# Stage one of a Fourier mixer on full rows: class r = 0 over 94 partitions, feature 128 from a padded matrix, front pieces one slot earlier, the last half tile in its own PSUM bank

## The chip, the cores and the metric

The kernel runs on one NeuronCore of a Trainium2 chip. The metric is the device time of one execution in microseconds. Before the change the median of three runs is 602.24 us (602.23 to 602.45).

## What is computed

The reference, cut to what matters:

```python
def _attn_ref(x):                                # x: (8, 3008, 256)
    X = np.fft.fft(x, axis=1)
    X = np.fft.fft(X, axis=2)
    return X.real.astype(np.float32)

def _moe_ref(x, w_tok1, w_tok2, w_ch1, w_ch2):   # d_tok 256, d_ch 1536
    h = np.maximum(x.transpose(0, 2, 1) @ w_tok1, 0.0) @ w_tok2
    u = x + h.transpose(0, 2, 1)
    h2 = np.maximum(u @ w_ch1, 0.0) @ w_ch2
    return (u + h2).astype(np.float32)
```

The input of the second function is the output of the first. Eight batches are worked on, one after the other; the whole computation is in 16-bit floats on the tensor engine (PE) with 32-bit sums in PSUM.

## The kernel before

**Two halves of work per batch.** The *front* of a batch makes the Fourier transform and the token mixer and ends in the tiles `ut` (the activations u, transposed). The *channel part* multiplies `ut` by the two channel matrices. While the channel part of batch b runs, the front of batch b + 1 is run in small pieces between its matmuls. The order on every engine is the order in which the program is written; nothing is rescheduled.

**The channel part** goes in six chunks of 512 positions per batch (the last has 448), and each chunk in four *slots*, s = 0 to 3. A slot has number 4c + s, from 0 to 23, and holds: three pairs of first channel matmuls (`mm1`, L763, into PSUM tiles `pc`, six matmuls of 512 or 448 columns; ACT takes them out with a ReLU, L766), and one quarter of the second channel product of the chunk before (`mm2`). Most chunks do `mm2` with a form of Strassen's scheme (`mm2_sums`, L804): its PSUM tiles are `px` and `py`, groups of 12 matmuls of 128 columns; `keep(i)` copies a part of px to `m` on ACT (L809); `residual` adds products and the input on the DVE or on POOL (L789); `block_sums` makes sums of blocks on the DVE (L780). A chunk at the end of an even batch, the first chunk and the very last one are *plain* (L863, PSUM tile `po`). The last tile of all is done in two halves of 128 columns so that the first half can be added and stored earlier; both halves lie in one `po` tile.

**The front** is a generator, and every `next` runs one piece. For batches 1 to 7 the pieces are, in order: six of `inner` (stage one for classes r = 1 to 15, five matmuls of 96 columns each, L511), two of `outer` (the edge pieces: class r = 0 by `edge`, L576 and L579, and class 16, L520), twelve of stage two (one `w` group each: L589 and L590 into `pw`, taken out by ACT, L307, and by the DVE, L592), two of `tok1` (L606, one for each half of the token features, with `units` on the DVE, L617 to L620, and `relu` on ACT, L629), `third(0)` (L638; `qs` on ACT, L641; two DVE operations into `yt`, L645), and then the pieces that make `ut`: two of `pu` (L723, added on the DVE, L731) for each chunk, and `third(1)` and `third(2)` in between. Numbered from 1 they are: 1 to 6 inner, 7 and 8 edges, 9 to 20 `w`, 21 and 22 `tok1`, 23 `third(0)`, 24 and 25 `pu` of chunk 0, 26 `third(1)`, 27 and 28 `pu` of chunk 1; the remaining nine run in the next iteration under `own_plan`.

`plan[b][slot]` says how many front pieces of batch b + 1 run in a slot. The first half of them (rounded down; none in a slot with s = 1) goes between `mm1` and `mm2`, the rest after `mm2`. `fold_plan` does the same for `fold`, the twelve DVE steps per batch that add the mirrored input rows and columns and fill the tile `eo` (L457 to L465) two batches ahead. Front pieces use a ring of three PSUM banks (tag "f"), `mm1` another three ("mm"), px, py and po the remaining two ("o2").

**Stage one.** `eo` has 94 partitions (`KR`; 47 is `NQ`): 47 for even and 47 for odd input groups. The tables `t1n` and `t1b` hold cosines and sines; in `t1n` the first part is masked by `mask0`, which is 1 on the first 47 partitions and 0 on the others. Class r = 0 needs only the first 47 rows, and the second feature half of the folded input needs, in its first output row, feature 128 in place of a zero. Before, `edge` takes both by slicing: 47 rows of `eo`, and a product with one single column (partition 0 of the output). Batch 0 has its own stage one (`fold0`, `zw0`, table `t0h`, L537).

Of the kernel before, what the change touches and what calls it, by code (L numbers as in the profile page):

```python
# [41 lines left out]
def kernel(  # L42
# [49 lines left out]
    def pvec(name, dt=FP32):  # L92
        return const.tile([P, 1], dt, tag=name, name=name)
# [249 lines left out]
    for o, h in ((shift0, half[0]), (shift1, half[1])):  # L343
        nc.vector.scalar_tensor_tensor(out=o[:], in0=h[:], scalar=-S / 4.0, in1=quart[:],
                                       op0=AT.mult, op1=AT.mult)
    mask0, q24 = pvec("mask0"), pvec("q24")
    ts(mask0[:], xicol[:], -1.0, AT.mult, 1.0, AT.add)
    ts(q24[:], qcol[:], 24.0, AT.add)
    t1n = const.tile([KR, 2, 2, 24], FP16, tag="t1n")
    t1b = const.tile([KR, 3, 24], FP16, tag="t1b")  # L350
# [4 lines left out]
    cs, v1 = (gen.tile([KR, 5, 24], FP32, tag=n, name=n) for n in ("cs", "v1"))  # L355
    reduced(v1[:], m1[:], m1[:], 47)
    sin(cs[:], m1[:], 47)
    t0h = gen.tile([NQ, 2, 24], FP16, tag="t0h")
    nc.scalar.activation(out=t0h[:], in_=cs[0:NQ, 0:4:2, :], func=AFT.Copy, scale=0.5)
    rest_of(vp, mp, S)  # L360
    table3(tp, vp)
    ident = const.tile([P, P], FP16, tag="ident")
# [4 lines left out]
    acol = pvec("acol")  # L367
    ts(acol[:], pcol[:], -1.0, AT.mult, 127.0, AT.add)
    ts(anti[:], jrow[:, 0:P], acol[:], AT.is_equal)
    for i, m in ((0, mask0), (1, xicol)):  # L370
        ts(t1n[:, :, i, :], cs[:, i:4:2, :], m[0:KR, :], AT.mult)
    ts(t1b[:, 1, :], cs[:, 4, :], float(np.sqrt(0.5)), AT.mult,
       xicol[0:KR, :], AT.mult)
    nc.vector.tensor_copy(out=t1b[:, 0:3:2, :], in_=t1n[:, :, 0, :])
    ixc = const.tile([P, 1], I32, tag="ixc")
    cfeat = pvec("cfeat")
    ts(cfeat[:], pcol[:], 1.0, AT.is_lt, -128.0, AT.mult)
# [19 lines left out]
    def tables_folded():  # L397
        pl.tensor_copy(out=td0[:], in_=tdu[:, 0:131])
        ts(td0[0:1, :], td0[0:1, :], 0.5, AT.mult, eng=pl)
        pl.tensor_copy(out=td1[:], in_=tdu[:, 131:WD])  # L400
        pl.memset(td1[0:1, 0:1], 0.5)
        pl.tensor_copy(out=alt[:], in_=altu[:, 0:131])
        pl.memset(alt[:, 130:131], 0.0)

    tcol, sgn = pvec("tcol"), pvec("sgn")
    perm = const.tile([P, P], FP16, tag="perm")
# [40 lines left out]
    def fold(b, engs):  # L447
        xp, xm = x_tiles.pop(b)
        eo = perb.tile([KR, NR, D], FP16, tag="eo", name="eo")
        state[b] = {"eo": eo}  # L450
        add, sub = AT.add, AT.subtract
        for s, (t0, t1) in enumerate(((13, 17), (9, 13), (5, 9), (1, 5))):
            tt = engs[s].tensor_tensor
            t = slice(t0, t1)
            rv = slice(16 - t0, 16 - t1 if t1 < 17 else None, -1)
            if s == 0:
                tt(out=xp[:, 1:NR, 0], in0=xp[:, 1:NR, 0], in1=xm[0:KR, ::-1, 0], op=add)  # L457
                tt(out=eo[:, :, 0], in0=xp[:, :, 0], in1=xp[:, :, 0], op=add)
            tt(out=xp[:, t, 1:D], in0=xp[:, t, 1:D], in1=xm[0:KR, rv, D - 1:0:-1], op=add)
            yield  # L460
            if t0 == 1:
                t = slice(0, t1)
            tt(out=eo[:, t, 1:129], in0=xp[:, t, 1:129], in1=xp[:, t, 255:127:-1], op=add)
            yield
            tt(out=eo[:, t, 129:256], in0=xp[:, t, 1:128], in1=xp[:, t, 255:128:-1],  # L465
               op=sub)
            yield


    def fold0():  # L470
        xp, xm = x_tiles.pop(0)
        eo = perb.tile([KR, NR, D], FP16, tag="eo", name="eo")
        state[0] = {"eo": eo, "xp": xp}
        tt, add = nc.vector.tensor_tensor, AT.add

        def mirror(t0, t1, lo, hi):
            rv = slice(16 - t0, 16 - t1 if t1 < 17 else None, -1)
            rd = slice(D - lo, D - hi if lo else None, -1) if lo else 0
            c = slice(lo, hi) if lo else 0
            t = slice(t0, t1)  # L480
            tt(out=xp[:, t, c], in0=xp[:, t, c], in1=xm[0:KR, rv, rd], op=add)

        r = slice(0, NQ)
        for t0 in (13, 9, 5, 1):
            if t0 in (13, 5):
                mirror(t0 - 4, t0 + 4, 0, 1)
            mirror(t0, t0 + 4, 1, D)
            yield
            if t0 == 13:
                nc.vector.memset(eo[r, 1, 0:1], 0.0)  # L490
                tt(out=eo[r, 0, 0:1], in0=xp[r, 0, 0:1], in1=xp[r, 0, 0:1], op=add)
                for i, op in ((0, add), (1, AT.subtract)):
                    tt(out=eo[r, i, 1:D], in0=xp[r, 0, 1:D], in1=xp[r, 0, D - 1:0:-1],
                       op=op)
                yield
# [34 lines left out]
    def zw0():  # L530
        st = state[0]
        eo, xp = st["eo"], st["xp"]
        z = perb.tile([P, 2, 24, 64], FP16, tag="z", name="z")

        def edge(pz, c):
            for i in range(2):
                nc.tensor.matmul(pz[:, 0:24], lhsT=eo[0:NQ, i, c], rhs=t0h[:, i, :],  # L537
                                 start=(i == 0), stop=(i == 1))

        for t0, e in Z0_ORDER:  # L540
            for half in range(2):
                if t0:
                    inner(xp, t0, half, z_put(z, half, t0, e[half]), ps_any)
                else:
                    outer(xp, half, z_put(z, half, 0, e[half]), edge,
                          ps_any)
                yield
        w = st["w"] = perb.tile([P, NG, WD], FP16, tag="w", name="w", bufs=2)
        for g in range(NG):
            pw = ps_any("pw")  # L550
            for lo, hi in ((131, WD), (0, 131)):
                for i, tab in ((0, tdu), (1, tdb)):
                    nc.tensor.matmul(  # L553
                        pw[:, lo:hi],
                        lhsT=z[:, i, 2 * g:2 * g + 2, :].rearrange("p a b -> p (a b)"),
                        rhs=tab[:, lo:hi], start=(i == 0), stop=(i == 1))
            copy(W0_COPY[g], w[:, g, :], pw[:, 0:WD])
            yield
# [4 lines left out]
    def front(b):  # L563
        st = state[b]
        if b == 0:
            yield from rest(b)
            return
        eo = st["eo"]
        z = perb.tile([P, 2, 24, 64], FP16, tag="z", name="z")
        for t0 in (11, 6, 1):  # L570
            for half in range(2):
                inner(eo, t0, half, z_put(z, half, t0, 0))
                yield
        for half in range(2):
            def edge(pz, c):
                nc.tensor.matmul(pz[:, 0:24], lhsT=eo[0:NQ, 0, c],  # L576
                                 rhs=t1n[0:NQ, half, 0, :], start=True, stop=True)
                if half:
                    nc.tensor.matmul(pz[0:1, 0:24], lhsT=eo[0:NQ, 0, P:P + 1],  # L579
                                     rhs=t1n[0:NQ, 0, 0, :], start=True, stop=True)  # L580

            outer(eo, half, z_put(z, half, 0, 0), edge)
            yield
        w = st["w"] = perb.tile([P, NG, WD], FP16, tag="w", name="w", bufs=2)
        for g in range(NG):
            pw = ps_f("pw")
            za = z[:, 0, 2 * g:2 * g + 2, :].rearrange("p a b -> p (a b)")
            zb = z[:, 1, 2 * g:2 * g + 2, :].rearrange("p a b -> p (a b)")
            nc.tensor.matmul(pw[:, 131:WD], lhsT=zb, rhs=td1[:], start=True, stop=True)  # L589
            nc.tensor.matmul(pw[:, 0:131], lhsT=za, rhs=td0[:], start=True, stop=True)  # L590
            copy(0, w[:, g, 132:WD], pw[:, 132:WD])
            nc.vector.scalar_tensor_tensor(  # L592
                out=w[:, g, 0:131], in0=alt[:], scalar=pw[:, 131:132],
                in1=pw[:, 0:131], op0=AT.mult, op1=AT.add)
            yield
        yield from rest(b)
# [247 lines left out]
    def mm2(b, c, c1, ks, box):  # L844
# [14 lines left out]
        o = D * (ks % 2)  # L859
        w = P if final and ks == 3 else D  # L860
        for d in range(0, D if n else 0, w):
            for ct in range(NCT):
                nc.tensor.matmul(po[0:n, o + d:o + d + w],  # L863
                                 lhsT=c1[:, ct, ks * P:ks * P + n],
                                 rhs=wc2[:, ct, d:d + w],
                                 start=(ct == 0), stop=(ct == NCT - 1))
            if final and ks == 3:
                j, p = ((lower, lower), (upper, turned_))[d // w]
                residual(nc.vector, osb[:, 3, j], po[:, o + d:o + d + w], rt[:, 3, p])
# [84 lines left out]

    plan = [[0] * 10 + [2] * 10 + [1, 2, 2, 3]] + [[1] * 13 + [0] + [2, 1] * 5] * (BB - 1)
    own_plan = [[2, 1, 1, 1, 1, 1, 1, 0, 1, 1, 0, 0, 1, 1] + [0] * 10,
                [1, 1, 1, 0, 0, 1, 1, 0, 1, 1, 0, 0, 1, 1] + [0] * 10]
    own_plan += [[1, 1, 1, 0, 0, 1, 1, 0, 1, 1, 0, 0, 1, 1] + [0] * 10] * (BB - 2)  # L960
    early_plan = [0] * 4 + [2, 2, 1, 2, 1, 2, 2] + [0] * 13
    fold_plan = [[0] * 8 + [1, 2, 0, 0] * 4 for _ in range(BB)]
    fold_plan[0] = [0] * 16 + [2, 2, 1, 0, 2, 2, 0, 0]
    fold_plan[1] = [1, 2, 0, 0] + [0] * 4 + [0, 2, 0, 0] + [1, 2, 0, 0] * 2 + [1, 2, 1, 0]
    prev = None
    turned_u = {(0, 0): turn_u(0, 0)}
    for b in range(BB):
# [90 lines left out]
```

## Time and profile before

| | before |
|---|---|
| median of three runs | 602.24 us |
| profiled execution | 602.5 us |
| span of its instructions | 600.7 us |
| granted TensorE clock | 0.998 |
| matmuls | 6325, busy 588.6 us |
| DVE busy | 449.7 us |
| ACT busy | 436.5 us |
| POOL busy | 141.2 us |

The span is counted from the first to the last instruction; the profiled execution has 1.8 us more around it. The busy time of matmuls overlaps, since they are pipelined, so the distance between the starts of neighbours says more than their duration. All times of places in the trace are microseconds from the start of the span. Iteration 0 runs up to about 102 us, and each further one takes about 71 us.

### The profile page before, as it was taken

What the parts mean: (1) busy time and instruction counts of PE and PEld (TensorE: products, weight loads), DVE (VectorE), ACT (ScalarE), POOL (GpSimd) and SP (SyncE); (2) the same over time, 40 slices, a digit from 0 to 9 for tenths busy, and PEclk for the clock granted to TensorE, in tenths of its full rate; (3) what the DMA queues carried; (4) which work ended last, traced back from release to release, by engine and by line L of the source; (5) the groups of instructions that cost most, each with busy time, mean ns of one, the idle gap of its engine ahead of it and who ended that gap; (6) DMA issues with size and microseconds to landing.
All of it is one profiled execution on the core that took longest, in us unless ns stands there. A gap on an engine that the chain in (4) does not pass through costs nothing.

```text
span 600.7 us, 15716 instructions
## 1 busy us (share of the span) xinstructions
PE 588.6 (98%) x6325; PEld 421.7 (70%) x6325; DVE 449.7 (75%) x1022; ACT 436.5 (73%) x984; POOL 141.2 (23%) x234
## 2 busy tenths in 40 slices
PE   6999999999999999999999999999999999999997
PEld 4846677667776677767777667766777777766675
DVE  8878697668796887659888687757879667676572
ACT  8776976777768777686777776777676867767772
POOL 7601322311142121311133112401211121111131
PEclk9999999999999999999999999999999999999999
DMA  9996961883539233953429432582232424233433
GB/s 149 211 182 126 137 98 38 153 122 53 87 61 174 54 76 67 152 72 88 73 50 165 96 64 55 98 160 53 55 89 46 81 53 97 47 70 70 83 60 100
DMA packets 86681, 56.53 MB, mean 94 GB/s; under 512 B 54944, under 2 KB 83552, under 8 KB 85856
## 3 DMA queue, kind: packets, MB, share of 16 engines
q1 hardware_dynamic: 77984, 37.77, 34.8%
q0 software_dynamic: 8320, 17.49, 17.0%
q8 instruction: 49, 0.80, 0.6%
q10 hardware_dynamic: 304, 0.26, 0.2%
q14 instruction: 24, 0.20, 0.1%
HBM read 34.98 MB, written 24.64 MB: 99 GB/s over the span
## 4 chain that ended last, share of the span: by engine, by line
PE 94%; DVE 3%; ACT 2%; issue 0%; POOL 0%; DVEq 0%; POOLq 0%
PE pc L763 40%; PE px L804 23%; PE py L804 9%; PE pu L723 7%; PE po L863 4%; PE pt L606 4%; PE pz L511 2%; PE py L638 1%; PE pq L638 1%; PE pw L589 1%; PE pw L590 1%; ACT z L307 1%; PE pw L553 0%; DVE sb L780 0%; ACT tt L307 0%; PE ph L428 0%
## 5 line engine op out<-in xcount | busy, mean ns | idle before, releaser
L766 ACT ACTIVATE c<-pc 128x512 f16<-128x512 f32 (+1 forms) x572 | 295.9, 595 | 36.6 <-PE pc L763 21.9
L789 POOL TENSOR_TENSOR osb<-osb,rt 128x256 f32<-128x256 f32 x84 | 78.9, 940 | 365.8 <-DVE osb L789 358.4
L763 PE MATMUL pc<-ut,wc1p 128*128 128x512 f16 x576 | 140.6, 379 | 0.5 <-DVE ut L305 0.5
L804 PEld LDWEIGHTS <-c 128*128 128x128 f16 x2016 | 121.4, 98 | 20.4 <-issue 1.2
L763 PE MATMUL pc<-ut,wc1m 128*128 128x512 f16 (+1 forms) x576 | 134.9, 370 | 0.0
L731 DVE TENSOR_TENSOR ut<-pu,yt 128x512 f16<-128x512 f32 (+1 forms) x94 | 63.3, 674 | 46.8 <-PE pu L723 46.0
L804 PEld LDWEIGHTS <-sb 128*128 128x128 f16 x1512 | 89.9, 98 | 10.3 <-issue 0.3
L809 ACT ACTIVATE m<-px 128x256 f32<-128x256 f32 x126 | 48.5, 385 | 66.2 <-PE px L804 43.5
L763 PEld LDWEIGHTS <-wc1p 128*128 128x128 f16 x576 | 52.1, 98 | 50.3 <-issue 2.5
L763 PEld LDWEIGHTS <-wc1m 128*128 128x128 f16 x576 | 52.9, 98 | 46.5
L804 PE MATMUL px<-wst,c 128*128 128x128 f16 x1008 | 70.0, 219 | 0.0
L804 PE MATMUL px<-wc,c 128*128 128x128 f16 x1008 | 63.1, 219 | 0.7 <-DVE osb L789 0.7
L780 DVE TENSOR_TENSOR sb<-sb,c 128x768 f16<-128x768 f16 x84 | 51.2, 609 | 2.9
L307 ACT ACTIVATE z<-pz 128x480 f16<-128x480 f32 (+1 forms) x60 | 39.7, 676 | 16.9 <-PE pz L511 11.0
L789 DVE TENSOR_TENSOR osb<-py,m 128x256 f32<-128x256 f32 x84 | 35.2, 419 | 21.4 <-ACT m L809 19.4
L723 PE MATMUL pu<-w2p,uu 128*128 128x512 f16 (+1 forms) x168 | 49.8, 379 | 0.0
L780 DVE TENSOR_TENSOR sb<-c 128x768 f16<-128x768 f16 x84 | 47.2, 561 | 2.4 <-ACT c L766 2.4
L780 DVE TENSOR_TENSOR c<-c 128x768 f16<-128x768 f16 x84 | 48.1, 572 | 0.0
L780 DVE TENSOR_TENSOR sb<-c,sb 128x768 f16<-128x768 f16 x84 | 47.1, 561 | 0.0
L592 DVE SCALAR_TENSOR_TENSOR w<-alt,pw 128x131 f16<-128x131 f16 x84 | 29.4, 351 | 20.2 <-ACT w L307 20.2
L645 DVE TENSOR_TENSOR yt<-py,qs 128x512 f16<-128x512 f32 x48 | 30.9, 686 | 17.7 <-ACT qs L641 17.6
L804 PE MATMUL py<-wc,sb 128*128 128x128 f16 x504 | 35.0, 219 | 0.0
(193 smaller groups left out, 673.7 us busy)
## 6 DMA issues: line engine op xcount, KB each, us to landing
out_dram<-osb SPq DMA_DIRECT2D x83, 256.0 KB, 3.9
xp<-in_x_dram POOLq DMA_DIRECT2D x16, 272.0 KB
out_dram<-osb SPq DMA_DIRECT2D x11, 192.0 KB, 3.9
xp<-in_x_dram POOLq DMA_DIRECT2D x16, 127.5 KB
rt<-ut SPq DMA_TRANSPOSE x96, 3.9
w2s<-in_moe_w_tok_dram POOLq DMA_DIRECT2D x1, 1504.0 KB
w1p<-in_moe_w_tok_dram POOLq DMA_DIRECT2D x4, 192.0 KB
wc<-in_moe_w_ch_dram POOLq DMA_DIRECT2D x1, 768.0 KB
```

The source lines that it names most:

```text
L307: nc.scalar.activation(out=out_, in_=in_, func=AFT.Copy)
L592: nc.vector.scalar_tensor_tensor(out=w[:, g, 0:131], in0=alt[:], scalar=pw[:, 131:132], in1=pw[:, 0:131], op0=AT.mult, op1=AT.add)
L606: nc.tensor.matmul(pt[:, o:o + n], lhsT=hw[:, g, th * P:th * P + P], rhs=w[:, g, f:f + n], start=(g == 0), stop=(g == NG - 1))
L645: nc.vector.tensor_tensor(out=yt[:, h, CW * c:CW * c + CW], in0=py[:], in1=qs[:], op=op)
L723: nc.tensor.matmul(pu[:, 0:n], lhsT=uu[:, th, int(minus), h, :], rhs=w2_cols(b, c)[:, th], start=(th == 0), stop=(th == 1))
L731: nc.vector.tensor_tensor(out=ut[:, h, 0:n].rearrange("p (a b) -> p a b", b=64), in0=pu[:, 0:n].rearrange("p (b a) -> p a b", b=64), in1=y ...
L763: nc.tensor.matmul(pc[:, 0:n], lhsT=wc[:, h, ct * P:(ct + 1) * P], rhs=ut[:, h, 0:n], start=(h == 0), stop=(h == 1))
L766: nc.scalar.activation(out=c1[:, ct, 0:n], in_=pc[:, 0:n], func=AFT.Relu)
L780: nc.vector.tensor_tensor(out=o, in0=x, in1=y, op=op)
L789: eng.tensor_tensor(out=o, in0=x, in1=y, op=AT.add)
L804: nc.tensor.matmul(o[:, t], lhsT=a(k)[:, f:f + P], rhs=w(k), start=(first and t == 0 and k == 0), stop=(k == HC - 1), skip_group_check=True)
L809: nc.scalar.activation(out=m[:, i], in_=pa[:, 0], func=AFT.Copy)
```

## The change

`edge` uses all 94 rows of `eo`, where the masked table `t1n` has zeros in the rows that don't belong to class 0 (for batch 0 the table `t0h` gets such a mask, `mask0h`, which is 0.5 or 0). Feature 128 is copied into column 0 of a matrix `nyq` that is otherwise zero, its place in `eo` is cleared, and a full matmul with `nyq` is summed into the same PSUM columns. The plan of the front pieces for batches 2 to 7 puts pieces 14 to 26 one slot (some half a slot) earlier; the fold steps of iterations 0 and 1 are placed a little differently. The second half of the last tile gets a PSUM bank of the front's ring.

```diff
-    ts(mask0[:], xicol[:], -1.0, AT.mult, 1.0, AT.add)
+    ts(mask0h[:], xicol[:], -0.5, AT.mult, 0.5, AT.add)
...
-    t0h = gen.tile([NQ, 2, 24], FP16, tag="t0h")
-    nc.scalar.activation(out=t0h[:], in_=cs[0:NQ, 0:4:2, :], func=AFT.Copy, scale=0.5)
+    t0h = gen.tile([KR, 2, 24], FP16, tag="t0h")
+    nc.scalar.activation(out=t0h[:], in_=cs[:, 0:4:2, :], func=AFT.Copy,
+                         scale=mask0h[0:KR, :])
...
+    ts(mask0[:], mask0h[:], 2.0, AT.mult)
...
+    nyq = const.tile([KR, P], FP16, tag="nyq")
...
+        pl.memset(nyq[:], 0.0)
...
             tt(out=eo[:, t, 1:129], in0=xp[:, t, 1:129], in1=xp[:, t, 255:127:-1], op=add)
+            if t0 == 1:
+                nc.vector.tensor_copy(out=nyq[:, 0:1], in_=eo[:, 0, P:P + 1])
+                nc.vector.memset(eo[:, 0, P:P + 1], 0.0)
             yield
...
-        r = slice(0, NQ)
+        r = slice(0, KR)
...
-                nc.tensor.matmul(pz[:, 0:24], lhsT=eo[0:NQ, i, c], rhs=t0h[:, i, :],
+                nc.tensor.matmul(pz[:, 0:24], lhsT=eo[:, i, c], rhs=t0h[:, i, :],
                                  start=(i == 0), stop=(i == 1))
...
-                nc.tensor.matmul(pz[:, 0:24], lhsT=eo[0:NQ, 0, c],
-                                 rhs=t1n[0:NQ, half, 0, :], start=True, stop=True)
+                nc.tensor.matmul(pz[:, 0:24], lhsT=eo[:, 0, c], rhs=t1n[:, half, 0, :],
+                                 start=True, stop=not half)
                 if half:
-                    nc.tensor.matmul(pz[0:1, 0:24], lhsT=eo[0:NQ, 0, P:P + 1],
-                                     rhs=t1n[0:NQ, 0, 0, :], start=True, stop=True)
+                    nc.tensor.matmul(pz[:, 0:24], lhsT=nyq[:], rhs=t1n[:, 0, 0, :],
+                                     start=False, stop=True)
...
         for d in range(0, D if n else 0, w):
+            if d:
+                po = ps_f("po")
...
-    plan = [[0] * 10 + [2] * 10 + [1, 2, 2, 3]] + [[1] * 13 + [0] + [2, 1] * 5] * (BB - 1)
+    plan = [[0] * 10 + [2] * 10 + [1, 2, 2, 3]] + [[1] * 14 + [2, 1] * 4 + [1, 1]] * (BB - 1)
...
-    fold_plan[0] = [0] * 16 + [2, 2, 1, 0, 2, 2, 0, 0]
-    fold_plan[1] = [1, 2, 0, 0] + [0] * 4 + [0, 2, 0, 0] + [1, 2, 0, 0] * 2 + [1, 2, 1, 0]
+    fold_plan[0] = [0] * 16 + [2, 2, 0, 0, 2, 2, 0, 0]
+    fold_plan[1] = [2, 2, 0, 0] + [0] * 4 + [0, 2, 0, 0] + [1, 2, 0, 0] * 2 + [2, 2, 0, 0]
```

More of the change, by code (lines that the diff above doesn't have):

```diff
@@ L345 @@
                                        op0=AT.mult, op1=AT.mult)
-    mask0, q24 = pvec("mask0"), pvec("q24")
-    ts(mask0[:], xicol[:], -1.0, AT.mult, 1.0, AT.add)
+    mask0, mask0h, q24 = (pvec(n) for n in ("mask0", "mask0h", "q24"))
+    ts(mask0h[:], xicol[:], -0.5, AT.mult, 0.5, AT.add)
     ts(q24[:], qcol[:], 24.0, AT.add)
```

## The prediction, as it was made

> **What bounds the kernel now.** First the busy shares (part 1) and the chain that ended last (part 4):
>
> ```profile
> PE 588.6 (98%) x6325; PEld 421.7 (70%) x6325; DVE 449.7 (75%) x1022; ACT 436.5 (73%) x984; POOL 141.2 (23%) x234
> PE 94%; DVE 3%; ACT 2%; issue 0%; POOL 0%; DVEq 0%; POOLq 0%
> ```
>
> The tensor engine is the bound, so a change counts by what it does to the distance from one matmul's start to the next. A busy time of one matmul (about 0.2 us) is mostly pipeline and says nothing of that distance. I subtracted starts along the PE timeline: 128 columns take 56 ns, 512 take 216, the 96-column L511 takes 42, the 12-column L526 takes 28. Everything above that pace adds up to some 15 us in the whole span, six of it before 32 us. What this change can gain is therefore in that small remainder. I looked for it in four places.
>
> The stage-one tile `pz`, by forms (duration min/median/max, first and last start, then rows*columns of the array):
>
> ```profile
> L511 PE MATMUL pz<-t1n,eo x210: 202/205/209, 59.4 to 475.7; 94*128 94x96 f16 x105
> L576 PE MATMUL pz<-t1n,eo x14: 182/183/184, 70.3 to 481.2; 47*128 47x24 f16 x14
> L520 PE MATMUL pz<-t1b,eo x14: 206/207/208, 70.4 to 481.4; 94*128 94x72 f16 x14
> L579 PE MATMUL pz<-t1n,eo x7: 170/170/170, 70.7 to 481.3; 47*1 47x24 f16 x7
> ```
>
> and the PE timeline around its two edge pieces in one batch:
>
> ```profile
> 193.29 0.83 PE L804 MATMUL px<-wst,c 128*128 128x128 f16 x12
> 194.05 0.18 PE L576 MATMUL pz<-t1n,eo 47*128 47x24 f16 x1
> 194.17 0.21 PE L520 MATMUL pz<-t1b,eo 94*128 94x72 f16 x1
> 194.21 0.39 PE L763 MATMUL pc<-ut,wc1p 128*128 128x512 f16 x1
> ...
> 196.18 0.83 PE L804 MATMUL py<-wc,sb 128*128 128x128 f16 x12
> 196.94 0.18 PE L576 MATMUL pz<-t1n,eo 47*128 47x24 f16 x1
> 197.06 0.17 PE L579 MATMUL pz<-t1n,eo 47*1 47x24 f16 x1
> 197.16 0.21 PE L520 MATMUL pz<-t1b,eo 94*128 94x72 f16 x1
> 197.20 0.39 PE L763 MATMUL pc<-ut,wc1p 128*128 128x512 f16 x1
> ```
>
> Twelve px matmuls need 12 x 56 = 0.67 us, so L576 could start at 193.96 and starts at 194.05. It then takes 0.115 for 24 columns, while L520 (72 columns) takes 0.04. In the second piece L576 comes 0.09 late and takes 0.113, L579 0.10. No engine is named as releaser: the loss sits wherever the number of rows or columns changes class (128 or 94 rows against 47; 128 columns against 1). Between 94 and 128 rows (L511, L520) nothing is lost.
>
> Then two places in slots 18 to 21 of the same pattern (a slot is a quarter of a chunk), and the DVE:
>
> ```profile
> 155.72 0.96 PE L606 MATMUL pt<-w,hp 128*128 128x130 f16 x12
> 156.05 0.35 DVE L592 SCALAR_TENSOR_TENSOR w<-alt,pw 128x131 f16<-128x131 f16 x1 [0.32 <-ACT w L307]
> ...
> 165.70 0.83 PE L804 MATMUL py<-wst,sb 128*128 128x128 f16 x12
> 166.05 0.42 DVE L789 TENSOR_TENSOR osb<-px,m 128x256 f32<-128x256 f32 x1
> 166.52 0.49 PE L804 MATMUL px<-wst,sb 128*128 128x128 f16 x6
> ```
>
> L606's twelve should be 11 x 57 + 220 = 0.85 us; they take 0.96, because the last reads the last `w` group, which L592 finishes only at 156.40. And px starts 0.82 after py where 0.67 is due: it waits for the DVE to read the px bank. Both recur in iterations 1 to 6 (0.11 and 0.15 each).
>
> Last, the chain of waits in iteration 0 and at the end:
>
> ```profile
> 87.00 0.42 DVE eo L463
> 88.63 0.34 DVE osb L789
> 89.01 1.00 PE px L804 x15
> ...
> 595.66 0.30 DVE osb L789
> 596.00 0.84 PE po L863 x12
> ```
>
> In iteration 0 the DVE is behind from 78.7 to 89.0 and the PE stands 0.82 us before 89.01. At the end the second half of the last tile waits until the DVE has read the first half.
>
> **What the Trainium skill says.** "TensorEngine Tiling (Array Packing)", Key Properties: "Mode switching requires drain"; 47 rows fall in its 64-row class, one column in a 32-column one. The trace agrees: 0.09 us at each of five switches per batch. "TensorE: Matmul & The Clock Gate", Back-to-back issue gap: warm, N/2.4 + 2.5 ns with a floor near 25 ns; the trace has 56, 42 and 28 ns. "PSUM — Partial Sum Buffer", PSUM bank collisions: a matmul may not write a bank that another engine is reading, whatever the columns; the wait at 595.66 is one.
>
> **The change, part by part.**
>
> *Edges.* The same number of matmuls, all with 94 rows and 128 columns. Old, from the last px or py start to the next L763: 152 + 115 + 39 = 306 ns and 152 + 113 + 102 + 39 = 406 ns (starts subtracted). New: 56 + 28 + 39 = 123 and 56 + 28 + 28 + 39 = 151, with 28 from L526 as the nearest row for 24 columns (bounds: 25, the floor, and 39, L520's). Gain 0.438 us a batch. In batches 2 to 7 nothing waits just behind: 6 x 0.438 = **2.63 us** (2.5 to 2.65). In batch 1 both edges lie at 70.2 to 70.8 and the PE then stands 0.37 us before 72.50 for the `z` copies, which ACT starts only after `w2p` (70.81) and `z` (71.53): I count 0 (bound 0.44). The four 47-row matmuls of batch 0 (14.9 to 15.3) are followed by 0.46 us of waiting for ACT's L287: 0 too (bound 0.35).
>
> *Front pieces one slot earlier (iterations 1 to 6).* The last `w` group is then followed by slot 18's six L763 (1.30 us) before the first L606: 6 x 0.11 = **0.66**. `third(0)` moves from slot 20 to the end of slot 19. With T its old place after slot 19: the DVE today idles 1.25 us for `qs` and starts `yt` at T+1.4, because ACT first works off slot 20's L766. Then yt 1.2, two sums 1.06, residual 0.42: too late for px. New: `qs` done about T+1.2, yt to 2.5, pu's add to 3.1, sums to 4.2, residual to 4.6; px is due at 0.45 + 1.14 + 0.43 + 1.34 + 0.43 + 1.14 + 0.67 = T+5.6. Margin 1.0 us: 6 x 0.15 = **0.91** gained. The same lateness costs 0.18 at 174.9 in iteration 1: **0.18**. Bounds of the three: all stay (0), all go (1.75). Piece 14 lands in slot 13, where the DVE has a gap of 0.8 us at 216.3 for its 0.26: nothing. No DMA moves, except that x loads follow the last fold step; a batch needs them eight slots (over 20 us) later.
>
> *Fold steps.* One L463 leaves slot 18 of iteration 0; its distance to the next DVE start is 0.34: the 0.82 us wait shrinks by **0.34** (0 to 0.43). In slot 0 of iteration 1, where a step arrives, the DVE has gaps of 0.5 us around 107: nothing. Two small DVE operations per batch are new (a 94x1 copy and a memset). Nearest rows: L617's 161 ns and L490's memset, 59; together 0.14 to 0.22 us in slot 21 (slot 10 for batch 1), taken out of the 1.0 us margin. Behind them stand one fold step and then slot 22's residual; px in slot 23 waits for that last. If the margin were gone they would cost up to 7 x 0.22 = 1.5 us.
>
> *Setup.* One 128x1 DVE operation more before `t1n` (at most 0.16, by its row), where the PE waits for ACT, not the DVE; `t0h` on 94 rows keeps its 242 ns; one POOL memset (about 0.1 to 0.3 us) ahead of loads that are wanted 15 us later. 0 (loss bound 0.16).
>
> *Last half tile.* Its matmuls follow at 56 ns instead of the 600 between 595.40 and 596.00: **0.54 us**; the DMAs behind it shift along. Nothing else holds an "f" bank then. Lower bound 0.3, if the two DVE adds queue up.
>
> Sum: 2.63 + 0.66 + 0.91 + 0.18 + 0.34 + 0.54 = 5.26 us against the profiled execution's 602.5 (span 600.7 and 1.8 around it), which gives 597.2; that run stood 0.26 above the median of 602.24, so **597.0 us**.
>
> **Rivals.** (1) *Only edges and end.* The DVE in slots 20 to 23 works without a gap today; the earlier pieces and the small operations might just move its waits. For: 163.8 to 175.4 is solid. Against: the 1.25 us it idles before. Gain 2.63 + 0.54 = 3.2: 599.1. (2) *The edges keep their gaps.* If the gap belonged to small matmuls and not to the row class, only the rest comes: 2.63, 599.6. Against: L526, 12 columns on 128 rows, takes 28 ns. (3) *Slower.* In slot 18 `tok1` now stands before mm2, so `relu` for half 0, which waits for the DVE's `uv`, is ahead of keep(2) in ACT's queue, and px in slot 19 needs keep(2). From the rows (uv, then three relus at 0.32 apart) keep(2) ends some 1.0 us before that px. It decides from 1.9 us of lateness: 0.88 x 6 then eats the 5.26. Two sums ahead of `uv` (1.06), one DVE step slowed as at 223.98 (1.18 instead of 0.68) and one more set of relus (0.82) make 2.4: px then stands 1.4 us in each of six batches, -5.26 + 8.4, 605.4. For: ACT today runs its L766 1.3 us late behind those relus in slot 19. Against: that margin.
>
> **How the numbers follow.** Own case 0.70, (1) 0.17, (2) 0.08, (3) 0.04, and 0.01 for a mixture near zero. The low end adds the two gains I put at nothing (5.26 + 0.79: 596.2); the high end takes in (1) and most of (2): 599.4. About 0.2% (1.2 us) is what a measurement of this kernel can tell from no change. Faster by more than that: own case, (1) and nearly all of (2), 0.94; slower: (3), 0.04; the rest 0.02.
>
> **What would show it.** After: every `pz` matmul with 94 rows and 128 columns, the first L763 0.74 us after the start of the twelve px ahead of the first edge (now 0.92) and 0.77 after that of the py ahead of the second (now 1.02); the twelve L606 of half 0 in 0.85 us; px 0.67 after py in slot 21; `po` x24 without a stand. Wrong would be: distances near 0.1 us still at the edges, or a new px or L763 wait on ACT `m` or DVE in slots 19 to 23 of every iteration.

## The result, and the profile after

The changed kernel takes **597.21 us** (median of four runs, 597.16 to 597.26). Measured alongside it, the kernel before took 602.35 us (median of four, 602.23 to 603.08); the ratio is 0.9912 with a 95% interval of 0.9895 to 0.9929. The profiled execution took 597.26 us, its span is 595.5 us at a granted clock of 0.999.

The busy shares on the page of the kernel after:

```profile
PE 582.6 (98%) x6325; PEld 420.0 (71%) x6325; DVE 450.0 (76%) x1037; ACT 437.4 (73%) x984; POOL 142.6 (24%) x235
```

The number of matmuls is the same and the tensor engine is still 98% busy. The kernel became faster although no busy share tells it. What shrank is the time between the starts of matmuls beyond the usual pace (56 ns for 128 columns, 109 for 256, 216 for 512 and so on): summed over the span, some 15 us before and 5.2 us less after.

The tile `pz` by forms in the kernel after; all forms now have 94 rows and 128 columns:

```profile
L583 PE MATMUL pz<-t1n,eo x14: 174/178/178, 70.4 to 476.9; 94*128 94x24 f16 x14
L527 PE MATMUL pz<-t1b,eo x14: 192/193/193, 70.4 to 476.9; 94*128 94x72 f16 x14
L586 PE MATMUL pz<-t1n,nyq x7: 173/173/173, 70.5 to 476.9; 94*128 94x24 f16 x7
```

The durations hardly moved (183 to 178 ns in the median for the first product). The starts did. The PE timeline of the kernel after, at the same two edges as before:

```profile
192.18 0.83 PE L811 MATMUL px<-wst,c 128*128 128x128 f16 x12
192.85 0.18 PE L583 MATMUL pz<-t1n,eo 94*128 94x24 f16 x1
192.88 0.19 PE L527 MATMUL pz<-t1b,eo 94*128 94x72 f16 x1
...
194.88 0.83 PE L811 MATMUL py<-wc,sb 128*128 128x128 f16 x12
195.55 0.18 PE L583 MATMUL pz<-t1n,eo 94*128 94x24 f16 x1
195.58 0.17 PE L586 MATMUL pz<-t1n,nyq 94*128 94x24 f16 x1
195.60 0.19 PE L527 MATMUL pz<-t1b,eo 94*128 94x72 f16 x1
195.64 0.38 PE L770 MATMUL pc<-ut,wc1p 128*128 128x512 f16 x1
```

From py's first start to the next first channel matmul there are 0.76 us now (195.64 - 194.88) against 1.02 before. Starts subtracted, L583 takes 30 ns, L586 26 and L527 32. The weight loads (PEld) show where the time was lost; the first line is of the kernel before, the second of the kernel after:

```profile
194.05 0.09 PEld L576 LDWEIGHTS <-eo 47*128 47x128 f16 x1
192.80 0.10 PEld L583 LDWEIGHTS <-eo 94*128 94x128 f16 x1
```

Before, the weights of the edge product were loaded only when the product itself started (both at 194.05). Now they are loaded 0.05 us ahead of it (192.80 and 192.85), while the last px matmul runs.

Slots 18 and 21 of iteration 2 (PE and DVE timelines of the kernel after):

```profile
225.04 0.85 PE L613 MATMUL pt<-w,hp 128*128 128x130 f16 x12
...
235.11 0.42 DVE L796 TENSOR_TENSOR osb<-px,m 128x256 f32<-128x256 f32 x1
236.01 0.83 PE L811 MATMUL py<-wst,sb 128*128 128x128 f16 x12
236.68 0.83 PE L811 MATMUL px<-wst,sb 128*128 128x128 f16 x12
```

L613 (L606 before) takes 0.85 us instead of 0.96, and px follows py after 0.67 us instead of 0.82. The DVE's `residual` ends at 235.53, 1.15 us before px needs the bank.

In iteration 0 and at the end (chain of waits, then the DVE timeline, kernel after):

```profile
88.44 0.34 DVE osb L796
88.82 1.22 PE px L811 x19
...
590.95 0.29 DVE L796 TENSOR_TENSOR osb<-po,rt 128x128 f32<-128x128 f32 x1 [0.18 <-PE po L872]
591.62 0.29 DVE L796 TENSOR_TENSOR osb<-po,rt 128x128 f32<-128x128 f32 x1 [0.38 <-PE po L872]
```

The stand of the PE before px near 89 is 0.49 us (0.82 before). The two additions of the last tile are 0.67 us apart, which is the twelve matmuls between them; before they were 1.21 apart (595.66 and 596.87).

One place went the other way. At the start the first product of stage one begins at 14.19 us instead of 13.74, and the first channel matmul 0.30 us later than before (32.28 for 31.98). The DVE and PE timelines of the kernel after:

```profile
10.38 0.27 DVE L97 TENSOR_SCALAR mask<-mask0h 128x1 f32<-128x1 f32 x1
10.75 0.24 DVE L97 TENSOR_SCALAR t1n<-cs,mask 94x48 f16<-94x48 f32 x1
...
14.19 0.60 PE L518 MATMUL pz<-t1n,xp 94*128 94x96 f16 x10 [0.49 <-DVE xp L488]
```

The new operation starts where `t1n` started before (10.36), and `t1n`, which reads its result, comes 0.39 us later. The PE now waits for the DVE's `xp` there, 0.49 us.

### The profile page after: what moved, and what is told of

Same layout as the page of the kernel before. It is cut to its first block, busy times and chain, and to the rows that moved or that the text cites. A ratio compares the mean times of both kernels' runs of the same rounds, so it can differ in the third digit from the quotient of the medians.

```text
span 595.5 us, 15730 instructions
## 1 busy us (share of the span) xinstructions
PE 582.6 (98%) x6325; PEld 420.0 (71%) x6325; DVE 450.0 (76%) x1037; ACT 437.4 (73%) x984; POOL 142.6 (24%) x235
## 3 DMA queue, kind: packets, MB, share of 16 engines
q1 hardware_dynamic: 77984, 37.77, 34.2%
## 4 chain that ended last, share of the span: by engine, by line
PE 94%; DVE 4%; ACT 1%; issue 0%; DVEq 0%; POOL 0%; POOLq 0%
PE pc L770 40%; PE px L811 23%; PE py L811 9%; PE pu L730 7%; PE po L872 4%; PE pt L613 4%; PE pz L518 2%; PE py L645 1%; PE pq L645 1%; PE pw L596 1%; PE pw L597 1%; ACT z L307 1%; PE pw L560 0%; DVE sb L787 0%; PE ph L432 0%; PE ph L430 0%
## 5 line engine op out<-in xcount | busy, mean ns | idle before, releaser
L811 PE MATMUL px<-wst,sb 128*128 128x128 f16 x504 | 35.0, 219 | 0.0
```

The costliest lines, as they stand in the source:

```text
L811: nc.tensor.matmul(o[:, t], lhsT=a(k)[:, f:f + P], rhs=w(k), start=(first and t == 0 and k == 0), stop=(k == HC - 1), skip_group_check=True)
```

## The experiments

Ten runs. Times are medians; the kernel before took 602.27 to 602.31 us in the same comparisons.

**1. The edges alone.** The plan, both fold plans and the bank of the last tile as before:

```diff
-    plan = ... [[1] * 14 + [2, 1] * 4 + [1, 1]] * (BB - 1)
+    plan = ... [[1] * 13 + [0] + [2, 1] * 5] * (BB - 1)
-            if d:
-                po = ps_f("po")
```

> The changed kernel with the plan of the front pieces, both fold plans and the PSUM bank of the last half tile as they were before: only the edges on 94 rows, the padded matrix and the table mask are changed. Own theory: the five changes of array class per batch cost about 0.09 us each, in the six batches with nothing waiting behind them: 6 x 0.46 = 2.8 us gained, less 0.1 to 0.3 at the start (one more DVE operation ahead of t1n) and less up to 0.4 where the two new DVE operations lengthen waits that the old plan still has; 599.7 to 600.1. Rival (small matmuls cost the same on any number of rows): no gain, 602.3 or a little more. Rival (the two DVE operations per batch cost their whole 0.2 us in each batch): 601.0.

Measured: **600.25 us** (ratio 0.9966, 0.9954 to 0.9979), 2.0 us gained, just outside the interval of the own theory. From iteration 3 on each batch gains 0.42 to 0.46 us, as expected. At the turn from iteration 1 to 2 most of one batch's gain is lost again: in slot 0 of iteration 2 the stand of px grew from 0.18 to 0.49 us, and a new one of 0.09 stands before py in slot 23 of iteration 1 (171.7). The timeline of this run, first the DVE in slot 22, then the place where px waits:

```profile
169.25 0.50 DVE L467 TENSOR_TENSOR eo<-xp 94x640 f16<-94x640 f16 x1
169.78 0.15 DVE L469 COPY nyq<-eo 94x1 f16<-94x1 f16 x1
...
170.05 1.29 DVE L652 TENSOR_TENSOR yt<-py,qs 128x512 f16<-128x512 f32 x2
...
174.92 0.41 DVE L796 TENSOR_TENSOR osb<-py,m 128x256 f32<-128x256 f32 x1
175.05 0.94 PE L811 MATMUL px<-wc,c 128*128 128x128 f16 x14 [0.32 <-DVE osb L796]
```

px waits for the DVE's last `residual`. The DVE works without a gap from `yt` to there. Between the starts of the fold step and of `yt` lie 0.80 us, where the kernel before has 0.41 (169.73 to 170.14): the two new operations take 0.39 us of the DVE here, which is what px and py lose (0.30 and 0.09). They are not hidden, because the old plan still keeps the DVE behind. In the later iterations of this run they are hidden even so, which rules out the rival that they cost their whole time in each batch. The small-matmul rival is out too.

**2. The plan alone.** The kernel before with the new `plan`.

> The kernel before with only the new plan of the front pieces. Own theory: the waits of L606 for the last w group (6 x 0.11), of px in slot 21 (6 x 0.15) and the single 0.18 go, and no new one comes: 1.75 us gained, 600.5; edges keep their gaps and the end its wait. Rival (the plan only moves the waits of the DVE-bound slots): 602.2 within 0.3, with new waits in slots 19 to 23. Rival (the plan pays only together with the shorter edges): below 1 us gained, above 601.3.

Measured: **600.59 us** (0.997, 0.9959 to 0.9981), 1.7 us gained. All waits of L606 at half 0, of px in slot 21 and the 0.18 at 174.9 are gone, no new one is in slots 19 to 23, and the edges keep their gaps of 0.09 us. Slot 21 of iteration 2 in this run:

```profile
237.52 0.83 PE L804 MATMUL py<-wst,sb 128*128 128x128 f16 x12
238.19 0.50 PE L804 MATMUL px<-wst,sb 128*128 128x128 f16 x6
```

px follows py after 0.67 us, with the edges as before. The start of this profiled execution was 0.4 us slow for a reason of its own (a wait of 0.63 that ends at 21.66), so the trace's own sum is smaller than the medians' difference. Both rivals are out.

**3. Fold steps and last bank alone.** The kernel before with the two `fold_plan` lines and `po = ps_f("po")`.

> The kernel before with only the two fold plans and the own PSUM bank of the last half tile changed. Own theory: the wait of 0.82 us in iteration 0 shrinks by 0.34 and the end comes 0.54 earlier: 601.4. Rival (at the end the stores, not the last product, set the time): 601.9. Rival (the fold step that leaves slot 18 is paid back in slot 0 of iteration 1): 601.7.

Measured: **601.29 us** (0.9982, 0.9975 to 0.9989), 0.98 us gained. In its trace the stand near 88 is 0.48 us, the two last additions follow each other as in the changed kernel (0.67 us apart), and the wait of 0.18 at 174.9 has shrunk to 0.05, since the last fold step of iteration 1 leaves slot 22. The last two additions:

```profile
595.05 0.29 DVE L789 TENSOR_TENSOR osb<-po,rt 128x128 f32<-128x128 f32 x1 [0.18 <-PE po L865]
595.72 0.29 DVE L789 TENSOR_TENSOR osb<-po,rt 128x128 f32<-128x128 f32 x1 [0.38 <-PE po L865]
```

So that small wait is taken away by the plan and, for the most part, by the fold steps alike; it must not be counted twice. Both rivals are out: the end came earlier by the whole 0.54 us, and slot 0 of iteration 1 shows no new wait.

**4 and 5. Sixty-four rows and sixty-five.** The changed kernel, with the edge products over fewer rows (the table is zero from row 47 on):

```diff
-nc.tensor.matmul(pz[:, 0:24], lhsT=eo[:, 0, c], rhs=t1n[:, half, 0, :],
+nc.tensor.matmul(pz[:, 0:24], lhsT=eo[0:64, 0, c], rhs=t1n[0:64, half, 0, :],
-nc.tensor.matmul(pz[:, 0:24], lhsT=nyq[:], rhs=t1n[:, 0, 0, :],
+nc.tensor.matmul(pz[:, 0:24], lhsT=nyq[0:64, :], rhs=t1n[0:64, 0, 0, :],
```

> The changed kernel with the edge products of batches 1 to 7 taken over the first 64 rows of eo, t1n and nyq in place of 94 (the rows from 47 on have zeros in the table). Theory that it is the row class: 64 rows belong to another class than 128, so each edge piece has a switch in and one out, four per batch at 0.09 us: 6 x 0.36 = 2.2 us lost against the changed kernel, 599.4, and the distances of L583 near 0.11 us again. Rival (the number of rows does not matter, the gain came from dropping the one-column product): within 0.2 of the changed kernel, 597.2. Rival (a cost that falls with each row more): between, since 64 is about a third of the way from 47 to 94.

> As the one with 64 rows, but over 65 rows. Theory of the row class: 65 rows need the 128-row class, so there is no switch and the time is that of the changed kernel, 597.2 within 0.1, with L583 at 30 ns. Rival (a cost that falls with each row more): practically as slow as with 64 rows, above 599.

Measured: **599.54 us** with 64 rows (0.9954, 0.9937 to 0.9971) and **597.18 us** with 65 (0.9915, 0.9898 to 0.9931). One row less costs 2.4 us, and 65 rows are as good as 94. The PE timelines of one edge, first with 64 rows, then with 65:

```profile
195.36 0.83 PE L811 MATMUL py<-wc,sb 128*128 128x128 f16 x12
196.13 0.18 PE L583 MATMUL pz<-t1n,eo 64*128 64x24 f16 x1
196.16 0.17 PE L586 MATMUL pz<-t1n,nyq 64*128 64x24 f16 x1
196.27 0.21 PE L527 MATMUL pz<-t1b,eo 94*128 94x72 f16 x1
```

```profile
194.78 0.83 PE L811 MATMUL py<-wc,sb 128*128 128x128 f16 x12
195.45 0.18 PE L583 MATMUL pz<-t1n,eo 65*128 65x24 f16 x1
195.48 0.17 PE L586 MATMUL pz<-t1n,nyq 65*128 65x24 f16 x1
195.50 0.19 PE L527 MATMUL pz<-t1b,eo 94*128 94x72 f16 x1
```

Two products of 64 rows in a row are 0.03 us apart, without a gap. The gaps come on the way from 128 to 64 rows (0.77 us from py's start, where 65 rows show 0.67) and from 64 to 94 (0.11, where 65 rows show 0.02). It is the change of class that costs, not the small product. A cost that falls with each further row is out, and so is the rival that only the one-column product mattered.

**6. One column again, on 94 rows.**

```diff
 nc.tensor.matmul(pz[:, 0:24], lhsT=eo[:, 0, c], rhs=t1n[:, half, 0, :],
-                 start=True, stop=not half)
+                 start=True, stop=True)
-nc.tensor.matmul(pz[:, 0:24], lhsT=nyq[:], rhs=t1n[:, 0, 0, :], start=False, stop=True)
+nc.tensor.matmul(pz[0:1, 0:24], lhsT=nyq[:, 0:1], rhs=t1n[:, 0, 0, :], start=True, stop=True)
```

> The changed kernel, with feature 128 again as a product with a single column (column 0 of nyq into the first output partition), but on 94 rows. Theory of classes: going from 128 columns to the one-column class and back is two switches per batch, with the rows left alone: 6 x 2 x 0.09 = 1.0 us lost, 598.2. Rival (only the number of rows matters): 597.2. Rival (a switch costs only when both rows and columns change): 597.2 too, with L586 at 26 ns.

Measured: **598.25 us** (0.993, 0.9913 to 0.9947), 1.04 us lost against the changed kernel. In the trace the way into the one-column product and the way out cost about 80 ns each, in each of the batches (starts subtracted, 108 and 106 ns where the changed kernel has 30 and 26):

```profile
195.64 0.18 PE L583 MATMUL pz<-t1n,eo 94*128 94x24 f16 x1
195.75 0.17 PE L586 MATMUL pz<-t1n,nyq 94*1 94x24 f16 x1
195.85 0.21 PE L527 MATMUL pz<-t1b,eo 94*128 94x72 f16 x1
```

A change of the columns alone, from 128 to one and back, costs nearly as much as one of the rows (0.075 to 0.096 us in the run with 64 rows). Where between one and 128 columns the boundary lies was not tried. Both rivals are out.

**7. Without the operation that makes `mask0`.** The changed kernel with

```diff
-    ts(mask0[:], mask0h[:], 2.0, AT.mult)
-    for i, m in ((0, mask0), (1, xicol)):
-        ts(t1n[:, :, i, :], cs[:, i:4:2, :], m[0:KR, :], AT.mult)
+    ts(t1n[:, :, 0, :], cs[:, 0:4:2, :], mask0h[0:KR, :], AT.mult, 2.0, AT.mult)
+    ts(t1n[:, :, 1, :], cs[:, 1:4:2, :], xicol[0:KR, :], AT.mult)
```

> The changed kernel without the DVE operation that makes mask0: the class-0 table is made from mask0h with a second multiplication by 2.0 in the same instruction. Theory (that operation pushed the DVE queue, and with it the first inner products, by 0.3 to 0.4 us; 0.11 of it is left after the first chunk): first pz again near 13.75 us instead of 14.19, and 0.1 to 0.3 us faster than the changed kernel: 596.9 to 597.1. Rival (the late start came from the input's transfers, not from the operation): 597.2 and the first pz at 14.0 or later.

Measured: **596.94 us** (0.9908, 0.9892 to 0.9925; 596.89 to 597.01 against the changed kernel's 597.16 to 597.26). The first product starts at 13.73 again:

```profile
10.37 0.24 DVE L99 TENSOR_SCALAR t1n<-cs,mask0h 94x48 f16<-94x48 f32 x1
...
13.73 0.60 PE L517 MATMUL pz<-t1n,xp 94*128 94x96 f16 x10
```

One operation on 128 single numbers cost 0.27 us of the whole kernel. The rival of the transfers is out.

**8. The copy into `w2p` later.** Run 7's kernel with, in iteration 0, `align_w2` behind the front pieces of its slot.

```diff
-                if b == 0 and sub < 16 and sub % 2:
-                    align_w2(sub // 2)
                 take(nxt, n - first)
+                if b == 0 and sub < 16 and sub % 2:
+                    align_w2(sub // 2)
```

> The changed kernel without the mask0 operation and, in iteration 0, with the copy into w2p issued after the front pieces of its slot instead of before them. Theory (in iteration 0 the PE stands 0.84 us at 72.5 because ACT copies w2p, 0.72 us, ahead of the two z copies; the edges' gain of that batch is hidden in this wait): the wait shrinks by about 0.7, and with the start's 0.1 to 0.3 the kernel takes 596.2 to 596.5. Rival (the DVE, late from 78.7 to 89.0, takes it back: the wait near 88 grows by as much): 597.0. Rival (a copy issued later delays the first L730 or the PSUM reads behind it): 597.2 or more.

Measured: **596.98 us** (0.9911, 0.9894 to 0.9927), the same as run 7. The wait at 72.5 did shrink, from 0.84 to 0.13 us. In its place came 0.20 us before the next first channel matmuls and 0.12 among them, and 0.36 before px at 77.4; the one near 88 grew by 0.03 only. The sum of these waits is 1.32 us for 1.33. The theory of a bad order falls, and so does the rival that the DVE near 88 takes it back: the waits came back within five microseconds. The way is that of the third rival, though its 597.2 was not reached. The chain of waits of this run goes from the copy to the PSUM reads (`c`) queued behind it on ACT, on through the DVE, and to px:

```profile
71.51 0.63 ACT w2p L307
72.14 1.46 ACT c L772 x3
...
77.41 0.61 PE px L810 x8
```

**9 and 10. The copies on POOL.** Run 7's kernel with the copies of slots 13 and 15, or that of slot 13 alone, on POOL:

```diff
-        copy(0, w2p[:, th, k, 0:NQ], w2v[:, th, k, :])
+        copy(2 if j in (6, 7) else 0, w2p[:, th, k, 0:NQ], w2v[:, th, k, :])   # or (6,)
```

> The kernel without the mask0 operation, with the last two of the eight copies into w2p (slots 13 and 15 of iteration 0) made by POOL instead of ACT. In the trace POOL has nothing to do from 71.3 to 77.9 us, while ACT works without a gap. Theory (ACT's own load between 70 and 77 is the bound of iteration 0 there, so that the order of its work moved the wait without shortening it): taking 1.4 us of copies from ACT removes the wait of 0.84 at 72.5; with what then is left 0.5 to 0.8 us faster than without this step: 596.1 to 596.4. Rival (POOL's copies of 752 elements slow the DVE, which is late from 78.7 on): 596.9 or more, and a longer wait near 88.

> As the run with two copies on POOL, with only the copy of slot 13 moved. Theory of ACT's load: the wait at 72.5 goes (0.7 to 0.8 us), the copy of slot 15 stays where it is and has no wait behind it in the trace: 596.1 to 596.4, as with two. Rival (only the two together free enough of ACT): 596.6. Rival (the DVE is slowed): 596.9 or more.

Measured: **597.25 us** with both copies (0.9916, 0.99 to 0.9933) and **596.75 us** with one (0.9908, 0.9892 to 0.9925; 596.71 to 596.78). Both miss their interval; one copy is a small gain over run 7 (0.2 us), two are a loss (0.3). Timeline of the run with one copy, and below it the same place in run 7:

```profile
70.62 1.81 DVE L786 TENSOR_TENSOR c<-c 128x768 f16<-128x768 f16 x1
71.21 0.80 POOL L305 COPY w2p<-w2s 128x752 f16<-128x752 f16 x1
72.49 0.51 PE L810 MATMUL px<-wst,c 128*128 128x128 f16 x6 [0.47 <-DVE c L786]
```

```profile
70.67 0.67 POOL L795 TENSOR_TENSOR osb<-osb,rt 128x256 f32<-128x256 f32 x1
70.70 1.07 DVE L786 TENSOR_TENSOR c<-c 128x768 f16<-128x768 f16 x1
```

The wait for `z` is down to 0.13 us, but the DVE's block sum beside the POOL copy takes 1.81 us, where the same one takes 1.07 in run 7, and px waits for it: a stand of 0.64 us is back. "SBUF — State Buffer" of the Trainium skill, Who interferes with whom, says that a DVE instruction with two SBUF inputs contends with a GpSimd instruction that reads SBUF. The traces agree: the 0.74 us more are close to the copy's 0.80. The 1.07 of run 7 hold such a delay already, since with POOL idle the same sum takes 0.55 (217.55 in the changed kernel). In both runs it ends 0.43 us after POOL's last instruction there (71.77 after 71.34, and 72.43 after 72.01), as if it had made hardly any headway until then. With two copies the second one (78.8 us) falls where the DVE is late already: the stand near 88 grows to 0.56 and one of 0.22 appears at 84. So the rival of the slowed DVE describes both traces; with one copy only, its 596.9 was not reached.

The kernel of run 10 is the fastest of all: 0.46 us ahead of the changed kernel.

## Why the prediction was right, point by point

597.0 us was forecast and 597.21 measured. Six of the seven steps agree one by one, so the total is not luck. The seventh, the setup, was wrongly set to nothing; with the 0.12 us that the edges gave more on the other side, it is about what the forecast is off by. By its own steps:

| step | forecast, us | measured, us | where from |
|---|---|---|---|
| edges, batches 2 to 7 | 2.63 | 2.75 | 6 x 0.46, chunk starts of before and after subtracted |
| last `w` group ahead of `tok1` | 0.66 | 0.66 | 6 x 0.11, trace |
| px in slot 21 | 0.91 | 0.91 | 6 x 0.15, trace |
| the wait at 174.9 | 0.18 | 0.18 | trace |
| fold step out of slot 18 | 0.34 | 0.33 | 0.82 to 0.49 |
| last half tile | 0.54 | 0.54 | last matmul start, less the gain up to there |
| setup | 0 (loss of 0.16 at most) | -0.27 | medians, run 7 against the changed kernel |
| sum | 5.26 | 5.10 | medians: 5.14 (5.03 from the 602.24 that the forecast started from) |

*Edges.* The mechanism is shown by the runs with 64 rows, 65 rows and one column: it is the change of class, at 0.075 to 0.096 us each. That the engine drains at such a change, as the prediction quotes, no run shows as such; the traces show the late weight load and the lost time. The term was a little too small because L527 (72 columns) takes 32 ns in the new surroundings where I had kept the 39 of the old ones. "TensorE: Matmul & The Clock Gate" of the Trainium skill, Back-to-back issue gap, which the prediction cites for the pace, gives that formula for an isolated matmul, and 81 and 131 ns for streams with 128 and 512 columns; the streams of these traces keep the formula (56 and 216 ns).

*Batch 1's edges and batch 0's four products at nothing.* Right. In iteration 0 the wait at 72.5 grew from 0.37 to 0.84 us, by the 0.47 that the edges in front of it gained. Behind batch 0's four products the next one starts at 15.84 in run 7 as it did before (15.83), though these pieces end 0.31 us earlier. Run 8 shows that the order of ACT's work is not what bounds this stretch: with another order the same time is lost a little later.

*Plan.* Right in both waits and in the margins: px in slot 21 had 1.15 us left where 1.0 was worked out. The third rival's place in the trace of after, ACT first, then PE:

```profile
228.31 0.36 ACT L816 ACTIVATE m<-px 128x256 f32<-128x256 f32 x1
...
229.75 0.83 PE L811 MATMUL px<-wst,c 128*128 128x128 f16 x12
```

keep(2) ends at 228.67, 1.08 us before the px that needs it (1.0 was forecast), behind the relus as described. A delay large enough to test the rival's price was not tried.

*The two DVE operations.* That they are hidden was right with the new plan, but their price was too low. They were put at 0.14 to 0.22 us, the sum of their durations; in the changed kernel they move the DVE's next start by 0.31 us in each batch (from 0.41 us after the fold step's start to 0.72), and in run 1, in the one stretch where the DVE is late, by 0.39, all of it lost by the PE. The copy reads what the fold step has just written and starts 0.03 us after its end, where before the next independent operation started 0.08 us ahead of that end. This is the one place where parts of the change depend on each other. The three parts alone gain 2.0, 1.7 and 1.0 us.

*Setup.* This term was wrong, though the total hardly shows it. I priced the new operation by its own duration (0.16 at most) and set it to nothing because the PE "waits for ACT, not the DVE". Both steps fail. The operation took 0.27 us, and `t1n`, which reads its result, started 0.10 us after its end, so the DVE's next start moved by 0.39 us. And the first product did wait for the DVE, in the kernel before already:

```profile
13.73 0.45 PEld L511 LDWEIGHTS <-xp 94*128 94x128 f16 x10 [0.22 <-DVE xp L481]
...
32.37 0.55 PEld L763 LDWEIGHTS <-wc1p 128*128 128x128 f16 x4 [1.23 <-DMA wc1p<-in_moe_w_ch_dram,ixc]
```

Only the copy of its result waited for ACT, by some 0.2 us: in the kernel after the copy starts 0.42 us after the product (14.61), so before it could have started at 14.16, and ACT was free at 14.36. A product 0.45 us later used this up. 0.30 us were left at the first channel matmul. The second line above shows why the two profiled executions don't tell the whole price: in that of the kernel before, the second channel matmul waited for a DMA until 32.37, so that at 34.2 only 0.11 us of the 0.30 remain. In run 7 that DMA has landed by 32.18. Its landing differs from execution to execution; the 0.27 us are the difference of the medians, whose ranges don't overlap.

Of the rivals, "only edges and end" and "the edges keep their gaps" are ruled out by runs 1, 2 and 4 to 6; "slower" found its queue order in the trace, but with a margin that holds.

## What to carry to other kernels

On an engine that is always busy, read the distance between the starts of neighbouring matmuls, not their durations: in this kernel a product cut to 47 rows or to one column saves nothing and costs 0.075 to 0.1 us on the way in and again on the way out, so pad it to the class of its neighbours (more than 64 rows here) and let zeros do the masking. Before calling an extra small operation free on an engine that does not bound the stretch, work out how far that engine is from bounding it, and what reads the result next: price it by how far it moves the next start, not by its duration. Moving work from a full engine to an idle one helps only if the two that then run side by side do not hold each other up.

## What was not expected of the hardware

The boundary of the row classes is sharp: 64 rows cost 2.4 us of this kernel and 65 nothing, with the same data. A DVE sum with both inputs in SBUF took 0.55 us with POOL idle, 1.07 beside one POOL addition and 1.81 with a POOL copy right behind that, and both times it ended about 0.43 us after POOL's last. A DVE operation of 0.15 us that reads the result just ahead of it, with a memset behind it, moved the DVE's next start by 0.31 to 0.39 us.
